# A fused attention and gated-MLP kernel: V's first column half in two transfers, a group's scaling and its turn behind separate dense parts

## The chip, the cores and the metric

The kernel runs on one core of one Trainium2 chip. A core has a matrix engine (TensorE, "PE" in the profile, with its weight loads listed as "PEld"), a vector engine (VectorE, "DVE"), a scalar engine (ScalarE, "ACT"), a general engine (GpSimd, "POOL") and SyncE ("SP"), whose queue issues nearly all of this kernel's DMA transfers; 16 DMA engines carry them. The metric is the device time of one execution in microseconds, the median of several runs.

## The reference

One layer norm feeds two blocks whose results are added to the input: causal attention with a window of 256 keys, 32 heads of 20 features, and a sigmoid-gated MLP.

```python
def _layernorm(x, axis=-1, eps=1e-5):
    m = jnp.mean(x, axis=axis, keepdims=True)
    v = jnp.var(x, axis=axis, keepdims=True)
    return (x - m) / jnp.sqrt(v + eps)

def reference(A_x, A_wqkv, A_wo, B_x, B_w_gate, B_w_up, B_w_down):
    def _A_ref(x, wqkv, wo):
        B, S, D = x.shape                      # 1, 2048, 640
        H = 32; Dh = D // H; W = 256
        qkv = (lambda x, *d: x.transpose(*d))((x @ wqkv).reshape(B, S, 3, H, Dh), 2, 0, 3, 1, 4)
        q, k, v = qkv[0], qkv[1], qkv[2]
        scores = jnp.einsum("bhqd,bhkd->bhqk", q, k) * (Dh ** -0.5)
        idx = jnp.arange(S)
        mask = (idx[:, None] - idx[None, :] >= 0) & (idx[:, None] - idx[None, :] < W)
        scores = jnp.where(mask[None, None], scores, -1e9)
        p = _softmax(scores, axis=-1)
        o = jnp.einsum("bhqk,bhkd->bhqd", p, v)
        return (lambda x, *d: x.transpose(*d))(o, 0, 2, 1, 3).reshape(B, S, D) @ wo

    def _B_ref(x, w_gate, w_up, w_down):       # 640 -> 1536 -> 640
        g = jnp.einsum("bsd,df->bsf", x, w_gate)
        u = jnp.einsum("bsd,df->bsf", x, w_up)
        h = _sigmoid(g) * u
        return jnp.einsum("bsf,fd->bsd", h, w_down)

    x = A_x
    xn = _layernorm(x, axis=-1)
    return x + _A_ref(xn, A_wqkv, A_wo) + _B_ref(xn, B_w_gate, B_w_up, B_w_down)
```

All inputs are bf16; sums are kept in float32 on the chip.

## The kernel before

The 2048 rows are worked in four chunks `c` of 512 rows (`CW`), each of four blocks of 128. The 640 model features lie in five chunks `d` of 128 on the partitions, so a projection is five matmuls that add up in one PSUM bank. Every instruction stands in an order written out by hand (`tc.manual_schedule()`): each engine works its own instructions in program order, and waits only where an operand or a buffer of another engine's is not ready.

**The start (lines 150 to 187 and 668 to 707).** SP's queue issues, in this order: rows 0, 1 and 3 of x's first chunk (`load_rows`, 160 KB each), `load_v(0)` (the first 320 of V's 640 weight columns, all five feature chunks, 400 KB), row 2, `load_v(1)` (the other 320 columns), the q weights and the k weights (800 KB each), and then MLP weights. Meanwhile each block of rows is normed (`xn`), turned on PE (`transpose_rows`, tile `pt`, five turns), and copied to `xnT`. PE's order is: turns of row 0, turns of row 1, the V projections `v00` (block 0, first column half) and `v10`, turns of row 3, `v01` (block 0, second column half), `v11` and `v30`, turns of row 2, and the rest of V. Then come the q and k projections of the first chunk (`g_qk(0)`, tile `pqk`). PE's first matmuls (`pwarm`) only keep the engine busy.

**The main loop.** For each chunk and each pair of head groups (a group is four heads that lie on four 32-partition strips; eight groups `g`, taken as four pairs `o`), `scores` makes the score matmuls (tile `ps`), ACT their exponentials (`pT`), POOL the masks (line 541). When all steps of a pair are done, `pv` multiplies with V (tile `acc`, two PSUM banks, one per group), and `finish_group` turns `acc` on DVE into `t1` (line 569). Then `scale_group` (line 575) makes the reciprocal of the sums (line 577), multiplies (line 581) into tiles `on` that gather 32 features each, and, when an `on` is full, turns it on DVE into a feature block `oc[c, m]` (line 585), which the output matmuls (`add_wo`, tile `y`) read as weights. A group has 20 features and a block 32 per strip, so a chunk's eight groups fill five blocks: groups 1, 3, 4, 6 and 7 fill one each, groups 0, 2 and 5 none.

**What fills PE between the scores.** A list of generators (`Fill`) holds the dense work: gate and up projections (`g_gu`: `pg`, `pu`, and `h` on DVE, line 458), the q, k, V projections of the next chunk, the norms of the next chunk (`g_norms`, ending in five DVE turns `turn` into `xnT`, line 298), and the outputs (`g_out`). Each `yield` with a cost is one "dense part", about five 512-column matmuls. `Fill.one` takes the next part and, behind it, the first entry of the list `behind`; where `hurry` is set (behind a chunk's last pair), two entries:

```python
                cost = next(gen)
                if cost and self.behind:
                    for _ in range(2 if self.hurry else 1):
                        if self.behind:
                            self.behind.pop(0)()
```

`finish_group` puts one entry per group into `behind`, the whole of `scale_group`, except for the last pair of all, where it runs at once. `flush` empties the list before the next `pv`. All dense work and `acc` share four PSUM banks (`ps_d`), so a bank is reused as soon as DVE or ACT has read it. `load_wd` (line 195) brings the MLP's down weights in five transfers during the first chunk.

Behind the first pair of the first chunk the dense parts are gate and up projections of chunk 0, with the turns of chunk 1 between them (`mix(g_gu(0, 4, 12), norms1, 0)`); the q projection of chunk 1 follows directly.

Of the kernel before, what the change touches and what calls it, by code (L numbers as in the profile page):

```python
# [9 lines left out]
P = 128  # L10
S = 2048
D = 640
# [3 lines left out]
DC = D // P  # L16
FC = F // P
CW = 512
# [7 lines left out]
HALF = 320  # L26
# [11 lines left out]
BF16 = mybir.dt.bfloat16  # L38
# [44 lines left out]
def pieces_of(g):  # L83

    f, left, src = g * DH, DH, 0
    while left:
        m, p = divmod(f, 32)
        n = min(left, 32 - p)
        yield m, p, src, n
        f, left, src = f + n, left - n, src + n  # L90
# [3 lines left out]
def kernel(  # L94
# [11 lines left out]
    nc = tc.nc  # L106
# [4 lines left out]
    def pool(name, bufs, **kw):  # L111
        return ctx.enter_context(tc.tile_pool(name=name, bufs=bufs, **kw))
# [11 lines left out]
    op = pool("op", 7)  # L124
# [17 lines left out]
    wqkv = [const.tile([P, DC + (part != "v"), D], BF16, name="w" + part) for part in "qkv"]  # L142
    wqkv_r = A_wqkv.rearrange("(c p) n -> p c n", p=P)
# [11 lines left out]
    def load_rows(s, queue):  # L155
        queue.dma_start(out=xc[0][:, s, :], in_=xr[:, s, :])  # L156

    def load_v(hf):
        a = hf * HALF
        nc.sync.dma_start(out=wqkv[2][:, :, a:a + HALF], in_=wqkv_r[:, :, 2 * D + a:2 * D + a + HALF])  # L160

    load_rows(0, nc.sync)
    load_rows(1, nc.sync)
    load_rows(3, nc.sync)
    load_v(0)
    load_rows(2, nc.sync)
    load_v(1)
    load_wqkv(0)
    load_wqkv(1)
# [24 lines left out]

    def load_wd():
        wd_r = B_w_down.rearrange("(c p) d -> p c d", p=P)
        for lo, hi in ((0, 3), (3, 6), (6, 8), (8, 10), (10, FC)):
            nc.sync.dma_start(out=wd[:, lo:hi, :], in_=wd_r[:, lo:hi, :])

    wo_i = tc.dram_tile([HG, NG * DH, D], BF16, name="wo_i")  # L200
# [261 lines left out]
    oc = {}  # L462
# [82 lines left out]
    def pv(c, o, parts):  # L545
        accs = [ps_d.tile([P, CW], FP32, name="acc", tag="d") for _ in range(2)]

        flat = sorted(((pt, *piece) for step, pt in parts for piece in step["pieces"]), key=lambda x: -x[3])
        late = [x for x in flat if SPAN - 1 == x[3]]
        rounds = ([x for x in flat if x[3] == SPAN], [x for x in flat if x[3] < 3], [x for x in flat if x[3] == 3] + late)  # L550
        flat = [x for r in itertools.zip_longest(*rounds) for x in r if x]
        for k, (pt, j, q, n, col) in enumerate(flat):
            kb, u = divmod(c * CW // U + j, 2)
            for a, acc in enumerate(accs):
                for i in range(HG):
                    h = o // 2 * HG + i
                    nc.tensor.matmul(  # L557
                        acc[32 * i:32 * i + 32, q * U:(q + n) * U],
                        lhsT=vt[kb][a * U:(a + 1) * U, u, h * VW:h * VW + 32],
                        rhs=pt[a * U:(a + 1) * U, i, col * U:(col + n) * U],  # L560
                        start=(k == 0), stop=(k == len(flat) - 1), skip_group_check=True)
        for a, acc in enumerate(accs):
            finish_group(c, o + a, acc)

    on = {}

    def finish_group(c, g, acc):
        t1 = np_.tile([P, 16, 32], FP32, name="t1")
        nc.vector.transpose(out=t1.rearrange("p b r -> p (b r)"), in_=acc)  # L569
        if c < NCH - 1 or g < NG - 2:  # L570
            fill.behind.append(lambda: scale_group(c, g, t1))
        else:
            scale_group(c, g, t1)

    def scale_group(c, g, t1):
        rec = np_.tile([P, 16, 1], FP32, name="rec")
        nc.vector.reciprocal(rec, t1[:, :, DH:VW])
        for m, slot, first, n in pieces_of(g):
            if slot == 0:
                on[m] = onp.tile([P, 16, 32], BF16, name="on")  # L580
            nc.vector.tensor_tensor(out=on[m][:, :, slot:slot + n], in0=t1[:, :, first:first + n],  # L581
                                    in1=rec.to_broadcast([P, 16, n]), op=MULT)
            if slot + n == 32:
                oc[c, m] = op.tile([P, CW], BF16, name="oc")
                nc.vector.transpose(out=oc[c, m], in_=on[m].rearrange("p b r -> p (b r)"))


    class Fill:
# [126 lines left out]
    fill = Fill()  # L715
# [13 lines left out]
    fill.add("x2", later(load_x, 2), 0)  # L729
    fill.add("wo_i", later(turn_wo), 0)  # L730
    fill.add("wd", later(load_wd), 0)
    fill.add("qk1", mix(g_qk(1), norms2, 6, 1, False), 50 * MM)
    fill.add("v1", mix(g_v(1), g_gu(1, 0, 2), 1, 2), 40 * 136 + 2 * GU)
# [17 lines left out]
    cuts = [(ends[n, NG - 2] + 2 + n, f"out{n}") for n in range(NCH - 1)] + [(len(todo), None)]  # L751
# [29 lines left out]
    c = NCH - 1  # L781
# [17 lines left out]
    cuts = (HALVES[0], (HALF, 4 * P), (4 * P, D))  # L799
# [45 lines left out]
```

## Time and profile before

| | us |
|---|---|
| three runs | 308.60, 308.23, 308.54; median 308.54 |
| the profiled execution | 308.19, span 306.5 |
| granted TensorE clock over the span | 1.00 |
| busy: PE, ACT, DVE, POOL | 299.8, 198.5, 177.6, 177.6 |
| DMA | 36.87 MB, 120 GB/s over the span |

The table of groups has the rows that matter for what the change touches: the duration of one, and how often it runs.

| line, engine, operation | count | mean ns |
|---|---|---|
| L569 DVE turn of acc into t1, 128x512 f32 | 32 | 697 |
| L577 DVE reciprocal, 128x16 f32 | 32 | 238 |
| L581 DVE multiply, 128x320 / 256 / 192 / 128 / 64 | 16 / 8 / 8 / 8 / 8 | 672 / 589 / 381 / 410 / 518 |
| L585 DVE turn of on into oc, 128x512 bf16 | 20 | 711 |
| L298 DVE turn of xn into xnT | 15 | 680 |
| L458 DVE h, 128x512 | 48 | 681 |
| L353 PE V projection, 128x320 | 160 | 300 (starts 136 apart) |
| L324 PE q, k projection, 128x512 | 191 | 380 (starts 216 apart) |
| L160 SP issue of V's weights | 2 | 434 |

How to read it: "span" is the time from the first to the last instruction on the core; the execution's own time has 1.7 us more around it. A matmul's duration includes the pipeline's depth, so matmuls overlap and their starts, not their durations, tell the rate. The weight loads (PEld) run ahead of their matmuls. In a list of waits, the columns are the time in all, how often, and the longest. In a timeline, they are the start, the time, the engine, line and operation, the tiles, shapes and how many, and in brackets the idle time before and what ended it. Completion times of a DMA transfer come from the trace's records of its 16 completion signals, one for each DMA engine.

### The profile page before, as it was taken

What the parts mean: (1) busy time and instruction counts of PE and PEld (TensorE: products, weight loads), DVE (VectorE), ACT (ScalarE), POOL (GpSimd) and SP (SyncE); (2) the same over time, 40 slices, a digit from 0 to 9 for tenths busy, and PEclk for the clock granted to TensorE, in tenths of its full rate; (3) what the DMA queues carried; (4) which work ended last, traced back from release to release, by engine and by line L of the source; (5) the groups of instructions that cost most, each with busy time, mean ns of one, the idle gap of its engine ahead of it and who ended that gap; (6) DMA issues with size and microseconds to landing.
All of it is one profiled execution on the core that took longest, in us unless ns stands there. A gap on an engine that the chain in (4) does not pass through costs nothing.

```text
span 306.5 us, 9993 instructions
## 1 busy us (share of the span) xinstructions
PE 299.8 (98%) x4279; PEld 164.9 (54%) x4314; DVE 177.6 (58%) x355; ACT 198.5 (65%) x197; POOL 177.6 (58%) x317
## 2 busy tenths in 40 slices
PE   7999999999999999999999999999999999999996
PEld 3654444445657654554557654554546665444775
DVE  5735539879675564496946464483733626372433
ACT  6923877698854649888674647878585547778000
POOL 3174687687982927676682728557382847557000
PEclk9999999999999999999999999999999999999999
DMA  7997987986427052810046212740000210000202
GB/s 204 362 326 255 305 202 214 316 243 217 144 91 170 21 180 70 256 58 2 2 132 130 66 58 83 242 137 0 2 2 2 69 42 25 2 2 2 88 21 68
DMA packets 40174, 36.87 MB, mean 120 GB/s; under 512 B 8992, under 2 KB 39840, under 8 KB 40096
## 3 DMA queue, kind: packets, MB, share of 16 engines
q1 hardware_dynamic: 39264, 35.45, 38.1%
q10 hardware_dynamic: 864, 0.77, 0.9%
q8 instruction: 34, 0.56, 0.7%
q14 instruction: 12, 0.10, 0.1%
HBM read 25.59 MB, written 11.44 MB: 121 GB/s over the span
## 4 chain that ended last, share of the span: by engine, by line
PE 96%; issue 1%; DMA 1%; ACT 1%; DVE 0%; SPq 0%
PE y L468 18%; PE pu L454 17%; PE pg L447 17%; PE pqk L324 14%; PE ps L524 9%; PE pv L353 8%; PE y L475 7%; PE acc L557 6%; DMA xc<-in_A_x_dram 1%; PE pt L277 0%; ACT xn L654 0%; ACT xn L659 0%; DVE xn L665 0%; SPq L156 0%; ACT rstd L660 0%
## 5 line engine op out<-in xcount | busy, mean ns | idle before, releaser
L541 POOL TENSOR_SCALAR_AFFINE_SELECT pT<-pT 64x512 bf16<-64x512 bf16 (+1 forms) x256 | 157.3, 614 | 83.0 <-ACT pT L530 70.6
L530 ACT ACTIVATE pT<-ps 128x2048 bf16<-128x2048 f32 (+1 forms) x76 | 141.0, 1855 | 59.5 <-PE ps L524 52.9
L458 DVE SCALAR_TENSOR_TENSOR h<-th,pu 128x512 bf16<-128x512 f32 x48 | 32.7, 681 | 49.7 <-PE pu L454 44.2
L454 PE MATMUL pu<-xnT,wu 128*128 128x512 bf16 x228 | 59.0, 380 | 0.7 <-issue 0.2
L447 PE MATMUL pg<-xnT,wg 128*128 128x512 bf16 x226 | 58.5, 380 | 0.9 <-issue 0.3
L468 PE MATMUL y<-wd,h 128*128 128x320 bf16 (+2 forms) x396 | 56.6, 295 | 0.0
L468 PEld LDWEIGHTS <-h 128*128 128x128 bf16 x396 | 36.8, 98 | 15.6 <-issue 1.8
L450 ACT ACTIVATE th<-pg 128x512 f32<-128x512 f32 x48 | 28.6, 595 | 15.5 <-PE pg L447 15.4
L447 PEld LDWEIGHTS <-wg 128*128 128x128 bf16 x240 | 22.3, 98 | 25.8 <-issue 2.0
L454 PEld LDWEIGHTS <-wu 128*128 128x128 bf16 x240 | 22.0, 98 | 25.5 <-issue 2.0
L524 PE MATMUL ps<-qT,kT 20*64 20x320 bf16 (+4 forms) x1440 | 32.1, 260 | 0.0
L569 DVE STREAM_TRANSPOSE t<-acc 128x512 f32<-128x512 f32 x32 | 21.1, 697 | 17.2 <-PE acc L557 17.2
L524 PEld LDWEIGHTS <-kT 20*64 20x64 bf16 x1440 | 15.4, 103 | 25.0 <-issue 22.4
L479 DVE SCALAR_TENSOR_TENSOR rows<-y,rows 128x320 bf16<-128x320 f32 x30 | 14.5, 488 | 22.5 <-PE y L475 22.4
L581 DVE TENSOR_TENSOR on<-t,rec 128x320 bf16<-128x320 f32 (+4 forms) x48 | 25.9, 540 | 1.1
L353 PE MATMUL pv<-wv,xnT 128*128 128x320 bf16 x160 | 25.8, 300 | 0.0
L475 PE MATMUL y<-wo,oc 128*128 128x320 bf16 (+2 forms) x165 | 24.2, 295 | 0.0
L324 PE MATMUL pqk<-xnT,wk 128*128 128x512 bf16 x97 | 23.0, 380 | 0.2
L324 PE MATMUL pqk<-xnT,wq 128*128 128x512 bf16 x94 | 22.7, 380 | 0.4 <-issue 0.2
L362 DVE CAST v<-pv 64x320 bf16<-64x320 f32 x29 | 14.1, 486 | 11.8 <-PE pv L353 11.6
L557 PE MATMUL acc<-pT,v 64*32 64x320 bf16 (+4 forms) x1440 | 19.7, 253 | 0.0
L557 PEld LDWEIGHTS <-v 64*32 64x32 bf16 x1440 | 16.2, 91 | 5.8 <-issue 1.6
(53 smaller groups left out, 194.8 us busy)
## 6 DMA issues: line engine op xcount, KB each, us to landing
qT<-sq SPq DMA_DIRECT2D x16, 256.0 KB
kT<-sk SPq DMA_DIRECT2D x16, 256.0 KB
sq<-st SPq DMA_DIRECT2D x20, 128.0 KB
sk<-st SPq DMA_DIRECT2D x20, 128.0 KB
out_dram<-rows SPq DMA_DIRECT2D x15, 160.0 KB
wg<-in_B_w_gate_dram SPq DMA_DIRECT2D x4, 480.0 KB
wu<-in_B_w_up_dram SPq DMA_DIRECT2D x4, 480.0 KB
xc<-in_A_x_dram SPq DMA_DIRECT2D x3, 640.0 KB
```

The costliest lines, as they stand in the source:

```text
L324: nc.tensor.matmul(ps, lhsT=wt[:, m, :], rhs=xnT[c][:, d, :], start=(d == 0), stop=(d == DC - 1))
L353: nc.tensor.matmul(ps[:, 0:HALF], lhsT=xnT[c][:, d, s * P:(s + 1) * P], rhs=wqkv[2][:, d, hf * HALF:(hf + 1) * HALF], start=(d == 0), stop ...
L447: nc.tensor.matmul(pg, lhsT=part(wg, d, f), rhs=xnT[c][:, d, :], start=(d == 0), stop=(d == DC - 1))
L450: nc.scalar.activation(out=th, in_=pg, func=TANH, scale=0.5)
L454: nc.tensor.matmul(pu, lhsT=part(wu, d, f), rhs=xnT[c][:, d, :], start=(d == 0), stop=(d == DC - 1))
L458: nc.vector.scalar_tensor_tensor(out=h, in0=th, scalar=1.0, in1=pu, op0=ADD, op1=MULT)
L468: nc.tensor.matmul(y[:, 0:cut[1] - cut[0]], lhsT=ht[c, f][:, s * P:(s + 1) * P], rhs=wd[:, f, cut[0]:cut[1]], start=(f == 0), stop=False)
L475: nc.tensor.matmul(y[:, 0:cut[1] - cut[0]], lhsT=oc[c, m][:, s * P:(s + 1) * P], rhs=wo[:, m, cut[0]:cut[1]], start=False, stop=(m == DC - 1))
L524: nc.tensor.matmul(ps[a * U:(a + 1) * U, i, col * U:(col + n) * U], lhsT=qk["k", kc, o // GH][32 * i:32 * i + DH, o % GH + a, kb * U:(kb + ...
L530: nc.scalar.activation(out=pt[:, :, 0:width], in_=ps[:, :, 0:width], func=EXP, scale=SCALE)
L541: nc.gpsimd.affine_select(out=view, in_=view, pattern=[[0, HG], [0, n], [sign, U]], compare_op=GE, fill=0.0, base=base, channel_multiplier ...
L557: nc.tensor.matmul(acc[32 * i:32 * i + 32, q * U:(q + n) * U], lhsT=vt[kb][a * U:(a + 1) * U, u, h * VW:h * VW + 32], rhs=pt[a * U:(a + 1) ...
```

## The change

Three places change. `load_v` takes cut points and issues a transfer for each stretch of feature chunks; the first column half is cut into chunks 0 to 2 and chunks 3 to 4, the second half stays one transfer. `load_wd` issues four transfers of three chunks each instead of five. `scale_group` becomes a generator: its first step makes the reciprocal and all multiplies of the group, and its second step, behind the `yield`, turns the blocks that became full. `finish_group` puts the two steps as two entries into `behind`; for the last pair of all it runs them one behind the other.

```diff
-    def load_v(hf):
+    def load_v(hf, cuts=(0, DC)):
         a = hf * HALF
-        nc.sync.dma_start(out=wqkv[2][:, :, a:a + HALF], in_=wqkv_r[:, :, 2 * D + a:2 * D + a + HALF])
+        for lo, hi in zip(cuts, cuts[1:]):
+            nc.sync.dma_start(out=wqkv[2][:, lo:hi, a:a + HALF],
+                              in_=wqkv_r[:, lo:hi, 2 * D + a:2 * D + a + HALF])
 
     load_rows(0, nc.sync)
     load_rows(1, nc.sync)
     load_rows(3, nc.sync)
-    load_v(0)
+    load_v(0, (0, 3, DC))
     load_rows(2, nc.sync)
     load_v(1)
...
     def load_wd():
         wd_r = B_w_down.rearrange("(c p) d -> p c d", p=P)
-        for lo, hi in ((0, 3), (3, 6), (6, 8), (8, 10), (10, FC)):
+        for lo, hi in ((0, 3), (3, 6), (6, 9), (9, FC)):
             nc.sync.dma_start(out=wd[:, lo:hi, :], in_=wd_r[:, lo:hi, :])
...
     def finish_group(c, g, acc):
         t1 = np_.tile([P, 16, 32], FP32, name="t1")
         nc.vector.transpose(out=t1.rearrange("p b r -> p (b r)"), in_=acc)
+        turns = scale_group(c, g, t1)
         if c < NCH - 1 or g < NG - 2:
-            fill.behind.append(lambda: scale_group(c, g, t1))
+            fill.behind.extend((lambda: next(turns), lambda: next(turns, None)))
         else:
-            scale_group(c, g, t1)
+            for _ in turns:
+                pass
 
     def scale_group(c, g, t1):
+        full = []
         rec = np_.tile([P, 16, 1], FP32, name="rec")
         nc.vector.reciprocal(rec, t1[:, :, DH:VW])
         for m, slot, first, n in pieces_of(g):
...
             nc.vector.tensor_tensor(out=on[m][:, :, slot:slot + n], in0=t1[:, :, first:first + n],
                                     in1=rec.to_broadcast([P, 16, n]), op=MULT)
             if slot + n == 32:
-                oc[c, m] = op.tile([P, CW], BF16, name="oc")
-                nc.vector.transpose(out=oc[c, m], in_=on[m].rearrange("p b r -> p (b r)"))
+                full.append(m)
+        yield
+        for m in full:
+            oc[c, m] = op.tile([P, CW], BF16, name="oc")
+            nc.vector.transpose(out=oc[c, m], in_=on[m].rearrange("p b r -> p (b r)"))
```

## The prediction

> **What bounds the kernel now.** I read the page first, then who waited for whom on TensorE (PE), then the chain of waits over the first microseconds, then the timelines of VectorE (DVE) and PE around each place that the change touches.
>
> From the page, the busy time and the chain that ended last:
>
> ```profile
> PE 299.8 (98%) x4279; PEld 164.9 (54%) x4314; DVE 177.6 (58%) x355; ACT 198.5 (65%) x197; POOL 177.6 (58%) x317
> ...
> PE 96%; issue 1%; DMA 1%; ACT 1%; DVE 0%; SPq 0%
> ```
>
> PE is the chain. All waits of PE, from the list of waits:
>
> ```profile
> PE pwarm L226 <- PEq L829: 0.8, 1, 0.8
> PE pt L277 <- DVE xn L271: 0.5, 1, 0.5
> PE pt L277 <- DVE xn L665: 0.4, 1, 0.4
> ```
>
> All three are over by 6.5 us. Since the ends of matmuls are modelled, I also took start-to-start distances from the trace: 0.216 us after a 512-column matmul and 0.136 after a 320-column one, nearly everywhere, and whole multiples of these where a record is missing. So after 13 us PE has no stall worth naming, DVE work that the change moves is hidden behind PE, and a DVE delay costs only what exceeds its slack. The stall that the first edit can reach stands at the start, in the chain of waits:
>
> ```profile
> 6.49 0.45 PE pt L277 x5
> 6.94 1.51 PE pv L353 x10
> 8.45 0.28 PE pt L277 x5
> 8.73 2.04 PE pv L353 x15
> ```
>
> The first five turns hold the chain for 0.45 us, the next five for 0.28: the first V matmul starts 0.16 us late (6.938 instead of the last turn's start 6.726 plus the usual 0.056). The trace's completion records say why: wv's first half is complete at 6.90, when the last of the 16 DMA engines reports.
>
> **The change, part by part.**
>
> *V's first half in two transfers.* The 400 KB become 240 (chunks 0 to 2) and 160. By the packets of this transfer, 40 of 640 bytes per engine at 0.032 us, the slowest engine would end the first part 16 packets (0.51 us) before 6.90, at 6.39. The second part is needed by the fourth matmul, 6.78 + 3 x 0.135 = 7.19, and lands at about 6.9. So the 0.16 us go. What is late next? After ten V matmuls the turns of rows 3 start at 8.293; 0.156 earlier is 8.137, and their xn, done at 8.085, allows 8.14 (xn to turn took 0.05 at 5.99 + 0.45 against 6.49): 0.15 us survive. Then comes v01, which reads V's *second* half:
>
> ```profile
> 8.52 1.92 PEld L353 LDWEIGHTS <-xnT 128*128 128x128 bf16 x15
> ```
>
> This weight load carries the wait for the second half, which is complete at 8.47: 0.05 us of slack today, and none with PE 0.15 us ahead. That wait takes the removed one's place: the load cannot run before 8.47 + 0.04 (the delay from completion to matmul at 6.90 and 6.94). Only the exposed load's overlap is left, matmul at about 8.53 instead of 8.572: a gain of 0.04 us.
>
> One more transfer also stands in front of the second half. SP issues it in 0.43 us (the wv rows), so row 2, V's second half, wq and wk are issued that much later. These issues have cover: the second half is issued at 3.22 but its data follow row 2's, which land from 6.0 to 7.35. On the engines, row 2 (160 KB) lands 0.45 us behind its predecessor and wq (800 KB) 2.22 behind its own; a straight line through both leaves 0.01 us per transfer beside the bytes. I take 0.01. Without the cover the second half lands 0.43 us later and the start loses 0.39. Row 2 feeds the turns at 10.61 through an xn done at 10.16, 0.4 us of slack; wq and wk land 2.2 and 5.2 us before their use. SP's later queue waits per transfer on the one eight earlier; those are the same transfers as before, save in the first eight and from wd on, all long complete. Start: -0.04, bounds -0.15 and +0.41.
>
> The Trainium skill (DMA: Bandwidth & Descriptors, Anatomy of one DMA) speaks against splitting: it charges a fixed cost of about 2.0 us per DMA, though fitted on another issue path, and calls most of it completion latency. The rows agree with latency, not with a serial charge; taken as serial it would be the second rival below.
>
> *w_down in four transfers instead of five.* Same bytes, one issue less; the last lands some 15 us before its use at 82 us. Nothing, and without that cover still one issue, 0.5 us, in its favour.
>
> *Scaling and turn apart.* Instruction counts on every engine stay, PE's, ACT's and POOL's order too; on DVE each group's turn (0.71 us, 20 of them) leaves the middle of the scaling. A pair of groups now takes four dense parts instead of two, and groups 0, 2 and 5 complete no block: their turn is empty and uses up a part. For the pairs that begin with group 0 or 2 the second scaling so falls behind a later dense part's DVE work, which waits for PE. At nearly all places the next reader on PE has over 0.9 us of slack or the DVE work ahead of it is the same. One is not so, group pair 0 of the first chunk, where x's next chunk is being turned:
>
> ```profile
> 47.17 0.69 DVE L458 SCALAR_TENSOR_TENSOR h<-th,pu 128x512 bf16<-128x512 f32 x1 [0.32 <-PE pu L454]
> 47.78 0.25 DVE L577 RECIPROCAL rec<-t 128x16 f32<-128x16 f32 x1
> 48.06 0.95 DVE L581 TENSOR_TENSOR on<-t,rec 128x320 bf16<-128x320 f32 x1
> 48.93 0.24 DVE L577 RECIPROCAL rec<-t 128x16 f32<-128x16 f32 x1
> 49.21 0.53 DVE L581 TENSOR_TENSOR on<-t,rec 128x192 bf16<-128x192 f32 x1
> 49.77 0.71 DVE L585 STREAM_TRANSPOSE oc<-on 128x512 bf16<-128x512 bf16 x1
> 50.41 0.30 DVE L581 TENSOR_TENSOR on<-t,rec 128x128 bf16<-128x128 f32 x1
> 50.63 0.68 DVE L458 SCALAR_TENSOR_TENSOR h<-th,pu 128x512 bf16<-128x512 f32 x1
> 51.23 1.29 DVE L298 STREAM_TRANSPOSE xnT<-xn 128x512 bf16<-128x512 bf16 x2
> 52.45 0.64 DVE L458 SCALAR_TENSOR_TENSOR h<-th,pu 128x512 bf16<-128x512 f32 x1
> 53.02 1.88 DVE L298 STREAM_TRANSPOSE xnT<-xn 128x512 bf16<-128x512 bf16 x3
> ```
> ```profile
> 48.38 1.25 PE L454 MATMUL pu<-xnT,wu 128*128 128x512 bf16 x5
> ...
> 54.69 2.33 PE L324 MATMUL pqk<-xnT,wq 128*128 128x512 bf16 x10
> ```
>
> DVE runs without a gap from 47.17 to the last xnT at 53.02 + 1.88 = 54.90. PE wants it at the fifth pqk matmul, 55.57: slack 0.67. In the changed order the h of 50.63 stands directly behind the multiply of 48.06. Its pu ends at 48.38 + 1.25 = 49.63, and h starts 0.11 after such an end (47.17 against a pu ended at 47.06): 49.74. DVE thus idles from 48.93 to 49.74, with the second scaling, the turn and five xnT turns, all the same work, queued behind: 0.81 us later. The last xnT ends at 55.71, PE may go on 0.05 later, and stalls 55.76 - 55.57 = 0.19 us. After it PE merely runs on, later. Bounds: the moved 128x192 and 128x128 multiplies took as little as 0.36 and 0.25 elsewhere, 0.22 less than here, and then there is no stall; the 128x128 one also took 0.72, 0.42 more: 0.61. I take 0.19, because POOL's masks run beside DVE there as before.
>
> A thinner cover: at 134.67 and 205.10 a V matmul now gets a PSUM bank read by a V copy on DVE, which ends 0.12 us ahead by the rows (without the turn in front of it). If that is gone it costs its excess, some 0.1 us each.
>
> *Sum*: -0.04 + 0.19 = +0.15 us. The profiled execution took 308.19 us, span 306.5 and 1.7 around it, 0.35 below the median of 308.54: so 308.34 against 308.19, and on the median **308.7**. A change of 0.2%, 0.62 us, is about what a measurement of this kernel can tell from none.
>
> **Rivals.**
>
> 1. *The start's gain is kept and the turn is hidden.* V's second half lands 0.15 us sooner than recorded here and the multiplies take their short times: -0.15 + 0 gives 308.4. For it: its 16 engines report from 7.12 to 8.47, so the last one alone sets the wait. Against: the bytes before it are the same. Still within 0.2%.
> 2. *Slower: V's second half comes late.* If the added transfer delays it by x, PE loses x - 0.04 at 8.5 us, plus 0.19 later; it decides, and passes 0.62 us, from x = 0.47. One SP issue or one landing distance (0.43 to 0.45) gives +0.6, 309.1; a serial charge as large as the first row's time from issue at 0.81 to landing at 3.14, 2.33, less the 0.45 seen between landings, gives x = 1.88 and 310.6. For it: 0.05 us of slack. Against: the 0.01 per transfer above.
> 3. *Faster: DVE in smaller pieces frees PE.* From a dense part to scores the starts lie 0.31 us apart, 0.09 more than usual, 51 times. Were these waits for DVE, one less for half of the 16 pairs would give 8 x 0.09 = 0.7 us, 307.8. Against: the 0.31 has no spread, as a wait would have.
> 4. *The split does not act*, because the stall at 6.94 was xnT's: +0.19 alone, 308.7. Against: the completion at 6.90.
>
> **How the numbers follow.** Forecast with rival 4: 0.55. Rival 1: 0.13. Rival 2, with other delays of its kind at thin covers (two banks, a 0.72 us multiply): 0.22. Rival 3: 0.10. Hence faster 0.10, same 0.68, slower 0.22. The bounds of the unknown costs reach from 308.4 to 309.6; the range 308.1 to 309.4 leaves out most of rival 3 and the heavy end of rival 2. The forecast's own range is 308.4 to 309.0.
>
> **What would show it.** Right: the first V matmul near 6.78; the load before v01 still at 8.5; DVE idle for some 0.8 us before the h near 49.7; the fifth pqk matmul of the second chunk about 0.2 us late; PE's distances elsewhere unchanged. Wrong: v01 well before 8.5 or well after 8.6, no DVE gap near 49 us, a new PE wait at 134 or 205 us, or fewer 0.31 us distances.

## The result, and the profile after

| | us |
|---|---|
| before, six runs of this comparison | median 308.35 (308.23 to 308.60) |
| after, six runs | median 309.62 (309.33 to 310.11) |
| ratio after / before | 1.0041, 95% interval 1.0028 to 1.0054 |
| profiled execution of after | 309.33, span 307.5 (before: 308.19, span 306.5) |

The changed kernel is slower by 1.27 us on the medians, and by 1.14 us between the two profiled executions. 308.7 was predicted, with 308.1 to 309.4 as its range: the sign of the sum was right, its size was not.

The page of after, its busy times and its chain that ended last:

```profile
PE 302.3 (98%) x4314; PEld 164.8 (54%) x4314; DVE 176.0 (57%) x355; ACT 198.5 (65%) x197; POOL 177.7 (58%) x317
...
PE 95%; DMA 2%; DVE 1%; SPq 1%; issue 0%
```

PE is still the chain, but a DMA now holds 2% of it: about 5.4 us from one transfer's issue to its landing. The list of PE's waits names the two places (columns: waiting line, what ended the wait, us in all, how often, longest):

```profile
PE pv L355 <- DMA wv<-in_A_wqkv_dram: 0.4, 1, 0.4
PE pqk L326 <- DVE xnT L300: 0.2, 1, 0.2
```

Neither was in the list before. The first is V's second half, by the chain of waits at the start (start, us, what):

```profile
3.70 5.40 DMA wv<-in_A_wqkv_dram
9.15 2.21 PE pv L355 x15
```

and by the timeline of PE's weight loads:

```profile
6.81 0.56 PEld L355 LDWEIGHTS <-xnT 128*128 128x128 bf16 x5
7.60 0.52 PEld L355 LDWEIGHTS <-xnT 128*128 128x128 bf16 x5 [0.24 <-DVE xnT L280]
8.22 0.35 PEld L279 LDWEIGHTS <-xn 128*128 128x128 bf16 x5
9.14 1.88 PEld L355 LDWEIGHTS <-xnT 128*128 128x128 bf16 x15 [0.58 <-DMA wv<-in_A_wqkv_dram]
```

The first load of V's projections comes at 6.81, its matmul at 6.86 instead of 6.94, directly behind the turns: the removed stall is gone. (The turns of row 1 themselves began 0.08 later here.) Then PE catches up with data that isn't there: v01's load, at 8.52 before, waits for the second half until 9.14. The completion records say the same: the second half's 16 DMA engines report from 7.05 to 9.10, where they reported from 7.12 to 8.47.

The second place is the one that the prediction worked out. DVE's timeline of after around the first pair of chunk 0:

```profile
47.76 0.69 DVE L460 SCALAR_TENSOR_TENSOR h<-th,pu 128x512 bf16<-128x512 f32 x1 [0.32 <-PE pu L456]
48.37 0.25 DVE L582 RECIPROCAL rec<-t 128x16 f32<-128x16 f32 x1
48.65 0.95 DVE L586 TENSOR_TENSOR on<-t,rec 128x320 bf16<-128x320 f32 x1
50.33 0.69 DVE L460 SCALAR_TENSOR_TENSOR h<-th,pu 128x512 bf16<-128x512 f32 x1 [0.73 <-PE pu L456]
50.93 0.25 DVE L582 RECIPROCAL rec<-t 128x16 f32<-128x16 f32 x1
51.21 1.02 DVE L586 TENSOR_TENSOR on<-t,rec 128x192 bf16<-128x192 f32 x2
52.16 0.70 DVE L593 STREAM_TRANSPOSE oc<-on 128x512 bf16<-128x512 bf16 x1
52.79 1.26 DVE L300 STREAM_TRANSPOSE xnT<-xn 128x512 bf16<-128x512 bf16 x2
53.97 0.65 DVE L460 SCALAR_TENSOR_TENSOR h<-th,pu 128x512 bf16<-128x512 f32 x1
54.55 1.88 DVE L300 STREAM_TRANSPOSE xnT<-xn 128x512 bf16<-128x512 bf16 x3
```

and PE's there:

```profile
55.28 1.04 PE L326 MATMUL pqk<-xnT,wq 128*128 128x512 bf16 x4
56.48 1.46 PE L326 MATMUL pqk<-xnT,wq 128*128 128x512 bf16 x6 [0.16 <-DVE xnT L300]
```

After group 0's multiply (48.65) DVE has nothing left in its order but the next `h`, and idles 0.73 us for its `pu`. The second group's scaling, its turn and five `xnT` turns stand behind. The last of them ends at 54.55 + 1.88 = 56.43, and the fifth `pqk` matmul, which could have run at about 56.14, runs at 56.48.

Laid over each other, weight load by weight load, the two traces differ in four steps: +0.59 at v01 (net of what PE had gained ahead of it), +0.32 at the fifth `pqk` matmul, +0.06 at 57.65 (before's time), +0.065 at 76.22. That is 1.03 us, and the spans differ by 1.0.

### The profile page after: what moved, and what is told of

Same layout as the page of the kernel before. It is cut to its first block, busy times and chain, and to the rows that moved or that the text cites. A ratio compares the mean times of both kernels' runs of the same rounds, so it can differ in the third digit from the quotient of the medians.

```text
span 307.5 us, 10032 instructions
## 1 busy us (share of the span) xinstructions
PE 302.3 (98%) x4314; PEld 164.8 (54%) x4314; DVE 176.0 (57%) x355; ACT 198.5 (65%) x197; POOL 177.7 (58%) x317
## 4 chain that ended last, share of the span: by engine, by line
PE 95%; DMA 2%; DVE 1%; SPq 1%; issue 0%
PE y L470 18%; PE pu L456 17%; PE pg L449 17%; PE pqk L326 14%; PE ps L526 9%; PE y L477 7%; PE pv L355 7%; PE acc L559 6%; DMA wv<-in_A_wqkv_dram 2%; DVE xnT L300 1%; SPq L156 1%; SPq L161 0%; DVE h L460 0%; DVE xn L481 0%; PE pt L279 0%
## 5 line engine op out<-in xcount | busy, mean ns | idle before, releaser
L456 PE MATMUL pu<-xnT,wu 128*128 128x512 bf16 x240 | 59.8, 380 | 0.0
L449 PE MATMUL pg<-xnT,wg 128*128 128x512 bf16 x240 | 59.8, 380 | 0.0
L586 DVE TENSOR_TENSOR on<-t,rec 128x320 bf16<-128x320 f32 (+4 forms) x48 | 24.3, 532 | 1.1
L355 PEld LDWEIGHTS <-xnT 128*128 128x128 bf16 x160 | 14.5, 98 | 9.3 <-issue 0.8
```

The costliest lines, as they stand in the source:

```text
L355: nc.tensor.matmul(ps[:, 0:HALF], lhsT=xnT[c][:, d, s * P:(s + 1) * P], rhs=wqkv[2][:, d, hf * HALF:(hf + 1) * HALF], start=(d == 0), stop ...
L449: nc.tensor.matmul(pg, lhsT=part(wg, d, f), rhs=xnT[c][:, d, :], start=(d == 0), stop=(d == DC - 1))
L456: nc.tensor.matmul(pu, lhsT=part(wu, d, f), rhs=xnT[c][:, d, :], start=(d == 0), stop=(d == DC - 1))
```

## The experiments

Twelve runs, each beside runs of before on the same chip. Theories: the split delays V's second half (S), the empty turn entries delay the last `xnT` (T). For S there are two readings. Either SP's later issue leaves the DMA engines short of work behind three small transfers (I), or every added transfer costs the engines time by itself (P). The expectations name their theories by letters of their own and say what each means.

### The split alone, twice

```diff
-    load_v(0)
+    load_v(0, (0, 3, DC))
...
-        for lo, hi in ((0, 3), (3, 6), (6, 8), (8, 10), (10, FC)):
+        for lo, hi in ((0, 3), (3, 6), (6, 9), (9, FC)):
```

`load_v` is that of the change; `scale_group` is that of before.

> V's first half in two transfers and w_down in four, the turn as before. Theory A (two separate mis-sized terms: in the changed kernel's profile the second half's wait costs 0.58 us at 8.5 us, the turn's order some 0.4 at 55 to 76 us): slower than before by 0.3 to 0.9 us, the weight load before v01 waiting for V's second half to about 9 us, the fifth pqk matmul of the second chunk unstalled. Theory B (the loss is all in the DVE order; the late second half of that profile was one slow packet and no rule): within 0.1 us of before, v01 at 8.5.

Measured: 309.47 (308.70 to 310.08, 7 runs) against 308.28, ratio 1.0035 [1.0023, 1.0048]. That is 1.19 us slower, beyond the 0.9 that was expected at most. The weight load of v01 in the profiled execution of 308.77:

```profile
9.11 1.88 PEld L355 LDWEIGHTS <-xnT 128*128 128x128 bf16 x15 [0.58 <-DMA wv<-in_A_wqkv_dram]
```

The same wait as in the changed kernel, no wait at `pqk`, and an end 0.56 us later than before's. So the split alone brings the first loss. But the profiled execution is near the lowest of its seven, so the same kernel was profiled again:

> The split alone once more, for a second profile: the first was of an execution of 308.77, while the median of its seven was 309.47. If the late second half is all of the split's loss, v01's weight load comes as much later than 8.52 as the end comes later than before's (306.5 of span), whatever the size: 0.5 to 1.6 us. If something else costs part of it, the end is later than v01's load is by 0.3 us or more, and another place shows a new wait.

```profile
8.65 1.88 PEld L355 LDWEIGHTS <-xnT 128*128 128x128 bf16 x15 [0.18 <-DMA wv<-in_A_wqkv_dram]
```

One run, 308.38 us against 308.27. Here the second half landed at 8.61 instead of 9.07. v01's load is 0.13 us later than before's, its matmul 0.09, and the end 0.19; 0.06 of the rest comes at 57.63. The landing of one and the same kernel thus scatters by half a microsecond, and the time goes with it: load at 8.65, 308.38 us; at 9.11, 308.77 us. No new wait stands anywhere else in the list. If v01's load alone made up the difference, the median of 309.47 would need a load near 9.8 (an estimate: 9.11 + 309.47 - 308.77); no execution with such a load was caught in a trace.

### The turn alone

`scale_group` and `finish_group` of the change, V's first half whole, w_down in five.

> The scaling and the turn apart, V's load and w_down as before. Theory A: slower than before by 0.4 to 0.5 us, all of it in the span between 55 and 77 us: 0.3 at the fifth pqk matmul of the second chunk and two times 0.06 behind it; V's start as before. Theory B: slower by 1.0 to 1.3 us, the whole difference.

Measured: 308.69 (308.49 to 309.07, 11 runs) against 308.28, ratio 1.0012 [1.0004, 1.0021]. In the profile, PE's timeline at the fifth `pqk` matmul:

```profile
54.58 1.04 PE L326 MATMUL pqk<-xnT,wq 128*128 128x512 bf16 x4
55.77 1.46 PE L326 MATMUL pqk<-xnT,wq 128*128 128x512 bf16 x6 [0.15 <-DVE xnT L300]
```

The step there is +0.32 and the one at 76.22 +0.07, as in the changed kernel; +0.4 in all, as the medians have it. At 57.65 there is no step. V's first half happened to land at 6.15 in this execution, without any split, so that PE was ahead by 0.11 at the start.

### The second entry only where a block fills

```diff
-            fill.behind.extend((lambda: next(turns), lambda: next(turns, None)))
+            fill.behind.append(lambda: next(turns))
+            if any(slot + n == 32 for _, slot, _, n in pieces_of(g)):
+                fill.behind.append(lambda: next(turns, None))
```

First on top of the changed kernel:

> The changed kernel, but a group that fills no block puts no empty second entry into the list. Theory A (the empty entry is what pushes the second scaling behind the next h): the DVE gap near 49 us and the stall at the fifth pqk matmul are gone, the start's loss stays: 0.3 to 0.5 us faster than the changed kernel, still 0.3 to 0.9 slower than before. Theory B' (the turn moved behind the scaling costs by itself): as the changed kernel.

Measured: 309.29 (308.57 to 309.54, 5 runs) against 308.28, ratio 1.0033 [1.0020, 1.0046]. In its profile the ten `pqk` matmuls run without the stall; the 1.01 us that stay are just above the 0.3 to 0.9 expected. Then with V's first half whole and w_down in five:

> Scaling and turn apart without the empty second entries, V's load and w_down as before. Theory A: no stall at the fifth pqk matmul of the second chunk, within 0.1 us of before (0.06 at 76 us may stay). Theory B' (the turn behind the scaling costs by itself): slower by 0.3 to 0.4 as with the empty entries.

Measured: 308.54 (308.15 to 308.81, 12 runs) against 308.50, ratio 0.9997 [0.9988, 1.0005]. DVE and PE of this kernel, the timelines at the same place:

```profile
48.59 0.95 DVE L588 TENSOR_TENSOR on<-t,rec 128x320 bf16<-128x320 f32 x1
49.45 0.24 DVE L584 RECIPROCAL rec<-t 128x16 f32<-128x16 f32 x1
49.73 0.97 DVE L588 TENSOR_TENSOR on<-t,rec 128x192 bf16<-128x192 f32 x2
50.62 0.67 DVE L460 SCALAR_TENSOR_TENSOR h<-th,pu 128x512 bf16<-128x512 f32 x1
```
```profile
55.22 2.33 PE L326 MATMUL pqk<-xnT,wq 128*128 128x512 bf16 x10
```

The second reciprocal again follows the first group's multiply, DVE doesn't idle, and the ten `pqk` matmuls run through. So the `pqk` stall comes from the empty entry and from nothing else in the turn's move. The step of 0.06 to 0.07 at 76.22 stays in both runs: a V copy on DVE stands there behind the same work in another order, which takes 2.46 us in the changed kernel (73.74 to 76.20) and took 2.39 before (72.78 to 75.17). Without the empty entry, moving the turn costs nothing that the comparison can tell, and gains nothing.

This execution also showed V's *whole* halves landing at 7.27 and 9.04, nearly as late as the latest split one, which cost it 0.5 us at the start. The landing scatters in the old form too; so S has to rest on medians and on several traces.

### One small transfer more, ahead of V

```diff
-    load_rows(3, nc.sync)
+    for a in (0, P // 2):
+        nc.sync.dma_start(out=xc[0][a:a + P // 2, 3, :], in_=xr[a:a + P // 2, 3, :])
```

V whole, the turn of before, w_down in four.

> Before, but row 3 comes in two transfers of 64 partitions each (same packets), so that V's second half has one more transfer in front of it as in the changed kernel, and w_down in four. V's first half stays whole. Theory A1 (one more transfer in the queue makes what follows late by itself, 0.3 to 0.6 us): the V half lands late too, slower than before by 0.3 to 0.6 us or more. Theory A2 (PE reaches v01 earlier in the split and meets the same landing; the lateness in one profile is scatter among the 16 engines): within 0.15 us of before.

Measured: 308.59 (308.21 to 309.02, 11 runs) against 308.28, ratio 1.0010 [1.0001, 1.0018]. SP issues the second half at 4.15, 0.93 later than before, and it still lands at 8.28 in the profiled execution, where v01's load isn't late. The cost is about 0.3 us on the medians, a quarter of the split's, and the profile, of the shortest of the eleven executions (308.21), can't show its place. In this trace a later issue alone doesn't make the landing late, then.

### Row 2 from ScalarE's queue

```diff
-    load_rows(2, nc.sync)
+    load_rows(2, nc.scalar)
```

The first activation is moved ahead of it and reads a constant of one. Once with the split, once with V's halves whole.

> The split alone, but row 2 is issued on ScalarE's queue (after its table load, at about 2.3 us), so that SP issues V's second half as early as before, at 3.2 us. Theory I (SP's issue, 0.5 us each, leaves the DMA engines short of work between 5 and 7 us: 270 GB/s there against 300 to 350 unsplit): the second half lands near 8.4 again, v01's load is not late, and the kernel is 0.1 to 0.3 us faster than before, some 1.2 faster than the split alone. Theory P (more and smaller transfers are slow in the engines themselves): the second half lands near 9.0, the kernel 0.5 to 1.2 us slower than before.

> Before, with row 2 on ScalarE's queue as in the first of these four, V unsplit. A control: V's second half lands some 0.4 us sooner than before if SP's issue limits it, at the same time if not. Its wait has slack there already, so the time is within 0.15 us of before either way, unless row 2 early delays V's first half (then up to 0.4 slower).

Measured: with the split 308.97 (308.71 to 310.44, 12 runs), whole 309.37 (309.20 to 309.55, 9 runs), against 308.50; ratios 1.0018 [1.0007, 1.0029] and 1.0029 [1.0020, 1.0038]. The experiment is spoilt in part: ScalarE issued row 2 at 0.86, ahead of nearly everything, so that it ran beside row 1, which landed at 4.27 and 4.39 instead of 3.56. The first V matmul came at 7.47 and 7.59 instead of 6.94 for that reason, and both lose another 0.32 us at a weight load that stands at 129.62 before, for which the profile names no cause. What it tells: with one SP issue fewer between the split halves and the second half, that lands at 7.99 (whole: 8.14), v01's load doesn't wait in either, and here the split kernel has the shorter median of the two, by 0.4 us, though the intervals overlap. The whole one lost 0.87 us, more than the 0.4 expected at most, and the split one 0.47, which neither reading had forecast. The Trainium skill (DMA: Bandwidth & Descriptors, Issuing engines are not separate DMA queues) says that transfers issued from different engines end up on the same 16 DMA engines and interleave there; row 1's 0.7 to 0.8 us agree.

### Where the extra cut stands

V's second half cut too:

```diff
-    load_v(0)
+    load_v(0, (0, 3, DC))
     load_rows(2, nc.sync)
-    load_v(1)
+    load_v(1, (0, 3, DC))
```

w_down in three transfers, the turn of before.

> Both column halves of V in two transfers (chunks 0 to 2, 3 to 4), w_down in three, the turn as before. v01 then needs only the second half's first part when it starts. Theory I: the first part lands some 0.5 us ahead of the whole, so most of the split's 1.1 us come back: -0.1 to +0.5 us against before, and another issue in the queue keeps wq and wk late without cost. Theory P: each further transfer costs 0.3 to 0.6 again, slower than before by 0.8 to 1.5.

Measured: 308.35 (308.12 to 309.19, 12 runs) against 308.50, ratio 0.9999 [0.9990, 1.0008]. PE's weight loads in v01:

```profile
8.46 0.40 PEld L355 LDWEIGHTS <-xnT 128*128 128x128 bf16 x4
9.20 1.45 PEld L355 LDWEIGHTS <-xnT 128*128 128x128 bf16 x11 [0.34 <-issue]
```

v01 starts on time with the first part (landed 8.42); its fourth matmul waits for the second part (complete at 9.16) and runs at 9.20 instead of 8.90, and the fifth load with it. Only 0.31 us are lost there, since three matmuls cover the rest. The first half is cut here as in the split alone, the second half lands as late (9.16), and the 1.19 us are gone from the median: what the split costs lies in v01's wait for the whole half. Only the second half cut, w_down in four:

> Before with V's second column half split (0, 3, DC) and the first left whole; w_down in four. One issue of SP is added behind every transfer that v01 needs first. If the first half's split hurt because SP issued the second half 0.5 us later into engines that ran short of work, the second half's first part is issued at 3.22 as before and lands before 8.47, v01's load stays at or before 8.55, and the time is 308.1 to 308.6, ratio 0.999 to 1.001. If each added transfer costs the engines time by itself wherever it stands, the second part lands near 9.1, the fourth v01 matmul waits for it, and wq lands near 11.3 instead of 10.7; the start loses about 0.2 to 0.3 us, since 0.4 us of it are covered by the three matmuls ahead.

Measured: 308.36 (308.14 to 309.38, 12 runs) against 308.37, ratio 0.9996 [0.9984, 1.0007]. The same with the turn, second entry only where a block fills:

> g1 with the changed turn, whose second entry is queued only where a block fills. If the two parts add up and g1 gains nothing or little, 308.1 to 308.6, ratio 0.998 to 1.001; no stall of the fifth pqk matmul. If the second entry itself costs something elsewhere, 308.7 or more.

Measured: 308.33 (308.16 to 308.54, 11 runs) against 308.37, ratio 0.9996 [0.9987, 1.0005]. In both, v01's load follows the turns without a wait, as reading I has it. One more transfer *behind* what v01 needs first costs nothing. (The first one's profiled execution, 309.38, is the longest of its twelve: PE stood still for 0.85 us at 84.0, and the profile names nothing that it waited for. The kernel with both halves cut lost 0.22 us at the same matmul; the w_down that it reads had landed by 69 in both. The last 16 KB load of instructions ahead of it began at 82.34 and 81.59 in these two traces and at 80.05 before, though PE was only 0.2 us later by then; that this is the cause isn't shown.) Neither is faster than before: there is no version here that beats it.

### The second half ahead of row 2

```diff
-    load_v(0)
-    load_rows(2, nc.sync)
+    load_v(0, (0, 3, DC))
     load_v(1)
+    load_rows(2, nc.sync)
```

> The split of V's first half as in the change, w_down in four, turn as before, but V's second half is issued ahead of row 2. If the late second half comes from small transfers that leave the engines short of work until SP issues the next, 400 KB issued at 3.2 fill the gap: the core moves over 300 GB/s from 5 to 7 us (346 and 303 before, 270 and 271 in the changed kernel), the second half lands at or before 8.0 and v01's load is not late; row 2 then lands near 8, its turns are late by 0.3 to 1.0 us, and the time is 308.5 to 309.5. If each transfer more costs the engines time by itself, 5 to 7 us stay near 270 GB/s, the second half lands near 8.6, and row 2 near 9, over 1.0 us late for its turns: 309.5 to 310.5.

Measured: 309.42 (309.06 to 309.69, 7 runs) against 308.37, ratio 1.0027 [1.0017, 1.0038]. The second half lands at 8.05, row 2 at 8.50. v01's load, at 8.47, is not late. The turns of row 2, at 10.61 before, are:

```profile
11.37 0.45 PE L279 MATMUL pt<-ident,xn 128*128 128x128 bf16 x5 [0.64 <-DVE xn L667]
```

a loss of 0.82 us net (0.77 later, and PE was 0.05 ahead until then), in the place of the one at v01. What this run is for stands in the windows from 5 to 7 us (columns: stretch, its length, busy time and instructions of PE, PEld, DVE, ACT and POOL, granted clock, DMA share, GB/s). Before, then after, then this kernel:

```profile
5.00:6.00 1.00, 0.65 (x7) 0.39 (x7) 0.88 (x4) 0.97 (x4) 0.00 (x0) 1.00 1.09 346
6.00:7.00 1.00, 0.59 (x8) 0.40 (x7) 0.96 (x4) 0.49 (x2) 0.00 (x0) 1.00 1.06 303
```
```profile
5.00:6.00 1.00, 0.57 (x7) 0.39 (x7) 0.91 (x3) 0.97 (x4) 0.00 (x0) 1.00 1.01 270
6.00:7.00 1.00, 0.59 (x9) 0.40 (x8) 0.93 (x4) 0.57 (x2) 0.00 (x0) 1.00 0.97 271
```
```profile
5.00:6.00 1.00, 1.00 (x9) 0.41 (x7) 0.89 (x3) 0.97 (x4) 0.00 (x0) 1.00 1.11 318
6.00:7.00 1.00, 0.60 (x9) 0.45 (x8) 0.95 (x3) 0.53 (x2) 0.00 (x0) 1.00 1.07 323
```

The last two columns are what the two readings differ in. The same transfers in the same number, with the 400 KB in the third place instead of row 2's 160 KB, move 318 and 323 GB/s where the changed kernel moves 270 and 271. This is as reading I has it and not as P has it. The rates of all traces, with the rate over the longer stretch from 3.6 to 7 us, and when the last of row 2 and V's second half had landed:

| kernel | order from V's first half on, KB | GB/s, 5 to 6 and 6 to 7 us | GB/s, 3.6 to 7 us | landed, us |
|---|---|---|---|---|
| before; the turn alone | 400, 160, 400 | 346, 303; 349, 312 | 271; 291 | 8.47; 8.39 |
| turn where a block fills, V whole | 400, 160, 400 | 332, 340 | 257 | 9.04 |
| one small transfer more, ahead of V | 400, 160, 400 | 324, 371 | 247 | 8.28 |
| only the second half cut; with the turn | 400, 160, 240, 160 | 356, 335; 353, 332 | 284; 279 | 8.56; 8.30 |
| second half ahead of row 2 | 240, 160, 400, 160 | 318, 323 | 271 | 8.50 |
| after | 240, 160, 160, 400 | 270, 271 | 263 | 9.10 |
| the split alone, twice | 240, 160, 160, 400 | 278, 263; 249, 288 | 264; 244 | 9.07; 8.61 |
| after, second entry where a block fills | 240, 160, 160, 400 | 227, 217 | 243 | 8.81 |
| both halves cut | 240, 160, 160, 240, 160 | 264, 272 | 269 | 9.16 |

From 5 to 7 us the five traces with 240, 160, 160 in a row lie at 217 to 288 and the seven without at 303 to 371. (The two with row 2 on ScalarE's queue have 287 and 334 with the split, 319 and 358 with V whole.) Over 3.6 to 7 us the groups overlap, 243 to 269 against 247 to 291: the split kernels moved more ahead of 5 us, after 251 GB/s from 3.6 to 5 us where before moved 194. So most of the difference between before and after from 5 to 7 us is a shift in time. Nor does the rate set the landing: 332 and 340 GB/s went with 9.04, 227 and 217 with 8.81. The landings tell the groups apart in all traces but one (8.61 to 9.16, against 8.28 to 8.56 and once 9.04). That the order of sizes counts more than the number of transfers is what these traces suggest; it isn't shown.

## Why the prediction was wrong

**The split.** Right: the stall at 6.94 was the first half's (after: V's first part landed at 5.96, the second at 6.42, and the first V matmul follows the turns at once), it was worth 0.16 us in PE's start, and it bought nothing, since v01's load holds the wait for the second half, with 0.05 us of slack. Wrong: the step "These issues have cover", with its 0.01 us per transfer. It took that number from a straight line through two landing distances of one trace and used it for a transfer that stands elsewhere in the queue. SP's queue of after:

```profile
2.18 0.96 SPq L161 DMA_DIRECT2D wv<-in_A_wqkv_dram  x2
3.19 0.47 SPq L156 DMA_DIRECT2D xc<-in_A_x_dram  x1
3.70 0.43 SPq L161 DMA_DIRECT2D wv<-in_A_wqkv_dram  x1
```

A transfer takes SP some 0.5 us, and 160 KB landed 0.45 us behind their predecessor (0.46 and 0.55 here), so there is little cover on this side; that this makes the landing late is reading I, argued and not shown. In the prediction's own terms x was 0.63 (9.10 instead of 8.47), not 0.01. The lateness grows from engine to engine: the first of the 16 reports the second half no later than before (7.05, before 7.12), their mean is 0.30 later (7.88, 7.58), the last 0.63. This is its second rival, by its mechanism and place and beyond the point (0.47) from which it was to decide, at 309.1 by the nearest size; it was given 0.22. In this trace the loss is 0.59; on the medians the split alone costs 1.19 (309.47 - 308.28), so of the 1.27 most is the split's.

**The scatter.** The prediction saw that the second half's 16 engines report over 1.35 us and that the last one sets the wait, and drew from it only a chance of a gain. A wait with 0.05 us of slack behind a landing that moved between 8.28 and 9.10 in eight traces that keep the order of the transfers and that half whole can only lose on average.

**w_down.** Its cost of nothing stands: two kernels with fewer transfers of w_down (four with only the second half cut, three with both halves cut) have ratios of 0.9996 and 0.9999.

**The turn.** Mechanism, place and chain were as predicted: DVE's idle time before `h`, which stands at 50.33 less the 0.59 of the start, 49.74 to the hundredth; PE going on 0.05 after the last `xnT`. The term was mis-sized, 0.32 for 0.19. The two moved multiplies took 52.16 - 51.21 = 0.95 us with what lies between them, where before they held DVE for 0.56 + 0.22 = 0.78; the prediction had bounded them (0 to 0.61) and taken the old value. Beside it, the thin covers at 134.67 and 205.10 held in this trace (the second cost 0.10 in the trace with the second half cut and the turn, close to the prediction's price), while another place, at 76.22, cost 0.065, which the prediction put under "over 0.9 us of slack or the DVE work ahead of it is the same". The step of 0.06 at 57.65 isn't the turn's: five traces with the turn of before have one of 0.05 to 0.08 there, and the turn alone has none. By medians the turn alone cost 0.41 (308.69 - 308.28).

**Rivals.** The third (DVE's pieces free PE) is out: the distances of 0.31 from a 512-column dense part to scores are as before, 42 of 42 in both traces, and the turn without the empty entry gains nothing (0.9997). The fourth is out too: the split did act on the stall at 6.94. The serial charge of the second rival is out: V's first two parts land 0.46 apart, what 160 KB took behind their predecessor before (0.45), not 2 us.

**The list of waits.** The prediction's "all waits of PE" leaves out three lines of the list, put down to "issue", 0.7 us in all; no term of its sum rests on them.

**What stays open.** The split's cost on the medians (1.19) is more than twice what its two traces show at their ends (0.19 and 0.56). Still later landings in the untraced executions would explain it, but none was seen; a stop of PE like the one at 84.0 could add to it. Nor is it settled why the second half lands late. Its later issue, the sizes ahead of it and the scatter of the 16 engines all bear on it, and no run here separates them; single packets that take 0.3 to 1.1 us, where the usual one takes 0.03, stand in the traces of both groups. And the two parts, 1.19 and 0.41, add up to more than the 1.27 of both; the intervals allow for that.

## What to carry to other kernels

Before a transfer is cut at the start of a kernel, look at who reads the transfer *behind* it, and with what slack: PE's gain ahead of a data wait is worth nothing, and whatever delay the added transfer brings is paid at that wait. If something must be cut, cut the transfer whose first part is needed next, not the one ahead of it: the same 240 and 160 KB were free in the second half and cost 1.2 us in the first. When work is made into several entries of a list that is served one per slot, count the empty entries: one that does nothing still pushes all behind it by a slot.

## What the runs showed of the hardware

- One SP issue of a DMA took 0.39 to 0.53 us at the start of after, and 160 KB followed their predecessor in 0.45 us before and in 0.46 and 0.55 us after. From 5 to 7 us the core moved 217 to 288 GB/s with 240, 160 and 160 KB in a row and 303 to 371 without, but over 3.6 to 7 us 243 to 269 and 247 to 291. The Trainium skill (DMA: Bandwidth & Descriptors, Rules for kernel authors) advises 1 MiB and more per DMA for bandwidth and names 64 KB as the size below which a DMA is mostly overhead; all these transfers lie between the two, and no run here shows where the overhead begins to count.
- The 16 engines of one transfer don't end together: V's second half reported over 0.49 to 2.06 us, and the last engine's landing in one and the same kernel moved from 9.07 to 8.61 between two executions. With 0.05 us of slack, whether PE waits for such a landing differs from execution to execution.
- A 128x320 multiply on DVE took 0.95 us with POOL's masks running beside it (48.65) and 0.49 us at 75.68 in the same kernel, where POOL has only a 128x4 operation; the line's mean of 568 ns hides this. That the masks are the cause was not tried by itself.
